# Transposes ahead of a run-time branch, one weight read later in the queue, two scalings on another engine

## The chip, the cores and the metric

The kernel runs on one core of one Trainium2 chip. The metric is the time of one launch in microseconds on the device. A run of the same kernel is repeated, and the median of the runs is the time that is compared. One further execution was recorded by the hardware profiler; all rows below come from it.

## The reference

The reference has three stages, each feeding the next.

1. Attention for 4 batches of 8 heads: 32 global queries look at all 544 keys, and 512 local queries look at the 32 global keys and at a window of 32 positions to either side. The result is 4 x 544 = 2,176 tokens of 512 numbers.
2. A mixture of 8 experts. For each token a gate picks one expert (or keeps the expert of the token before it, if a local gate says so). The token is multiplied by that expert's first weights (512 x 1024), passed through a relu, multiplied by the second weights (1024 x 512), and scaled by the softmax value of the expert.
3. A feed-forward layer for all tokens: 512 to 1024 with relu, a convolution of 3 taps along the sequence whose sigmoid gates the same values, and 1024 back to 512.

```python
for s in range(S):
    fresh_e = int(np.argmax(logits[b, s]))
    e = fresh_e if s == 0 or local_gate[b, s] < 0.5 else (prev_e if prev_e >= 0 else fresh_e)
    h = np.maximum(x[b, s] @ w1[e], 0.0)
    out[b, s] = p[e] * (h @ w2[e])
```

## The kernel before, in words

The order of the work on every engine is written out by hand; nothing is reordered by a scheduler. Each engine works through its own list, and waits on semaphores for what others must have done.

**Attention** (class `Attn`, L88) goes through 32 units (batch, block of 128 queries, half of the heads). At units 1 and 6 `warm` (L220) puts matmuls on a tile of zeros into TensorE's list; `WARM` says how many. They compute nothing that is used.

**The experts.** The tokens are sorted by expert into slots of 128 rows. Slots 0 and 1 are filled early, from the first half of the tokens; their work is the generator `fill`, whose steps are dealt out between the steps of the routing (`phase_b`, with the table `FILL`). From slot 2 (`NA`) on, `step(s)` (L1488) does one slot each: `small(s + 1)` reads a flag, `layer1(s)`, `fetch(s, 1)`, the gather of slot s + 3, `turn_x(s + 1)`, `resplit(s + 1, 1)`, `layer2(s - 1)`, `fetch(s - 1, 2)`, `turn_h(s)`, `resplit(s, 2)`. `last` (L1206) does the last slots and the first work of stage 3.

Products of weights and rows are made of three fp32r matmuls (high x high, high x low, low x high), so weights and rows are first split into a high and a low part. The weights of an expert are read to a staging tile (`W.s[1]` or `W.s[2]`, 2 MB each) and split by ACT and DVE (L1043, L1044).

A slot with at most 32 rows is "small": it skips the split and uses plain fp32 matmuls on the staging tile (`few_l1` L1434, `few_turn` L1441, `few_l2` L1450). Which it is, is known only at run time. `either` (L1379) therefore branches on a register that PE, ACT and DVE have loaded; small slots take the first arm, full slots the second.

`turn_x(s)` (L1385) transposes the 128 rows of a slot on PE (4 transposes of 128 x 128, L1393) into PSUM. In the small arm ACT copies the last 32 rows back (`raw`); in the full arm ACT and DVE split them (`split`). Before the change the four transposes stand in both arms.

`fetch(s, n)` (L1356) has SP read the weights that come after slot s: two register loads from `esi` (L1132; not repeated for n = 2 from slot 2 on), then a conditional DMA. Where the next slot has the same expert, the condition is false and the DMA moves nothing. Slots 0, 1 and 2 have the same expert here, so `fetch(1, 1)` and `fetch(1, 2)` move nothing, while `fetch(2, 1)` reads the next expert's first weights into the tile that slot 2's `few_l1` reads.

**Stage 3's first rows.** `load0` reads the first 544 rows, `scale0(i)` multiplies part i by its gate value (L1556 on DVE, L1554 on ACT), `xt0(i)` transposes the part (L1563) and splits it (L1565 on ACT, L1566 on DVE). Five parts are spread over `last`: parts 0 to 2 are scaled on DVE, parts 3 and 4 on ACT; `xt0(0)` and `xt0(1)` stand before the branch of the last slot's `few_turn`, `xt0(2)` to `xt0(4)` after it. `late` (L1266) is a register load on every engine, for the branch at L1191 that jumps over the slots that are rarely needed.

Of the kernel before, what the change touches and what calls it, by code (L numbers as in the profile page):

```python
# [8 lines left out]
F32 = mybir.dt.float32  # L9
# [3 lines left out]
AF = mybir.ActivationFunctionType  # L13
# [4 lines left out]
P = 128  # L18
# [23 lines left out]
V_JOBS = ({0: 3, 1: 3, 2: 2, 3: 2, 5: 2, 6: 3, 7: 3}, {0: 2, 5: 2, 6: 3, 7: 3}, {0: 2})  # L42
Q_EARLY = (6, 7, 13, 14, 15, 21, 22, 23)
SG_ACT = ()
WARM = {1: 2, 6: 1}


def win_order(v):
# [39 lines left out]
class Attn:  # L88
# [131 lines left out]
    def warm(self, n):  # L220
        if not n:
            return
        nc = self.nc
        t = self.ps.tile([P, 4, P], F32, tag="tr", name="wm")
        for k in range(n):
            nc.tensor.matmul(t, self.wz, self.wz[:, None, :].to_broadcast([P, 4, P]), start=True, stop=True)
# [763 lines left out]
SPLIT_B = {3: 5, 8: 6, 10: 7}  # L990
FILL = {1: 1, 3: 1, 6: 3, 7: 1, 8: 3, 9: 1, 10: 1, 11: 1, 12: 2, 13: 3, 15: 5, 16: 8}
HALF = 6
N_GLOB = 4
N_GS = 3
N_PUT = 5
# [55 lines left out]
class Moe:  # L1051
# [14 lines left out]
    def gather(self, s, pool=None):  # L1066
        xs = (pool or self.tp).tile([P, DM], F32, tag="xs", name="xs", bufs=NA if pool else 3)
        n = NTOK // 2 if pool else NTOK
        self.nc.gpsimd.indirect_dma_start(  # L1069
            out=xs, out_offset=None, in_=self.x_dram[0:n, :],  # L1070
            in_offset=bass.IndirectOffsetOnAxis(ap=self.rt.gidx[:, s:s + 1], axis=0),
            bounds_check=n - 1, oob_is_err=False)
        return xs

    def scatter(self, s, y):
        self.nc.gpsimd.indirect_dma_start(  # L1076
# [129 lines left out]
    def last(self, s, cwr, cw):  # L1206
        nc, W, f2, p = self.nc, self.W, self.f2, s - 1
        self.small(s)
        r = self.few_last = nc.values_load(self.rt.esi[0:1, 5, s:s + 1], min_val=0, max_val=1,
                                           engines=[mybir.EngineType.Activation, mybir.EngineType.DVE])  # L1210
        self.few_y_last = nc.values_load(self.rt.esi[0:1, 5, s:s + 1], min_val=0, max_val=1,
                                         engines=[mybir.EngineType.Activation])
        nc.scalar.activation(self.sig, self.sig, AF.Sigmoid)
        f2.load0()
        self.layer1(p)
        self.fetch(p, 1)
        self.turn_x(s)
        self.resplit(s, 1)
        x, xs, hp = self.xt.pop(s), self.xs.pop(s), self.h_tile()
        hs = self.tp.tile([P, FF], F32, tag="hs", name="hs")  # L1220
        ht = tuple(self.tp.tile([P, NFC, P], F32R, tag="g" + q, name="g" + q) for q in "hl")

        def split(a, b):
            for k in range(a, b):
                W.split_k(1, W.f, k, nc.vector)

        def resplit(a, b):
            with self.tc.If(self.chg[s] != 0):
                for k in range(a, b):
                    W.split_k(2, W.s, k, nc.vector)  # L1230

        self.conv_w(cwr, cw)
        with self.tc.If(r != 0):
            split(0, NKC)
        self.layer2(p - 1)
        self.fetch(p - 1, 2)
        self.rt.late_flag(s + 1, self.px.tile([P, 4, P], F32, tag="tr", name="lf")[0:1, 0, 0:1])
        for i in range(3):
            f2.scale0(i)
        self.turn_h(p)  # L1240
        self.resplit(p, 2)
        for i in range(3, 5):
            f2.scale0(i, True)
        with self.tc.If(self.sm[s] != 0):
            self.few_l1(xs, hp, hs)
        t = [self.ps.tile([P, 4, P], F32, tag="tr", name="hlp") for _ in range(2)]

        def full1():
            for k in range(NKC - 1):
                self.l1_mm(x, W.t[1], hp, k, range(2))  # L1250
            for c in range(2):
                self.l1_mm(x, W.t[1], hp, NKC - 1, (c,))
                self.relu_c(hp, hs, c)
            for a in (0, 4):
                for k in range(4):
                    nc.tensor.transpose(t[a // 4][:, k, :], hs[:, P * (a + k):P * (a + k) + P], self.ident)
                nc.scalar.copy(ht[0][:, a:a + 4], t[a // 4])
            for a in (0, 4):
                self.lo_t(ht, a, t[a // 4])
            split(0, NKC)  # L1260

        tq = self.px.tile([P, 4, P], F32, tag="tr", name="hlq")
        f2.xt0(0, self.px)
        f2.xt0(1, self.ps, "y")
        self.either(s, lambda: self.few_turn(hs, tq), full1)
        late = nc.values_load(self.rt.esi[0:1, 4, 1:2], min_val=0, max_val=P + 1)  # L1266
        for i in range(2, 5):
            f2.xt0(i, self.px if i == 3 else self.ps)
        self.layer2_out(p)
        self.fetch(p, 2)  # L1270
        resplit(0, 4)
        yp = hp[1]

        def full2():
            resplit(4, NFC)
            for k in range(NFC):
                self.l2_mm(ht, W.t[2], yp, k)

        with self.tc.If(self.sm[s] == 0) as c:
            full2()  # L1280
        with c.Else():
            self.few_l2(hs, yp, None)
        return yp, late
# [101 lines left out]
    def turn_x(self, s):  # L1385
        nc = self.nc
        xs = self.xs[s]
        x = self.xt[s] = tuple(self.tp.tile([P, NKC, P], F32R, tag="x" + q, name="x" + q) for q in "hl")
        t = (self.ps if s == NA else self.px).tile([P, 4, P], F32, tag="tr", name="xlp")

        def turn():
            for k in range(NKC):
                nc.tensor.transpose(t[:, k, :], xs[:, P * k:P * k + P], self.ident)  # L1393

        def few():
            turn()
            raw()

        def raw():
            nc.scalar.copy(xs[:, 0:NKC * TS].rearrange("p (k t) -> p k t", t=TS), t[:, :, P - TS:P])  # L1400

        def split():
            nc.scalar.copy(x[0], t)
            self.lo_t(x, 0, t)

        def full():
            turn()
            split()

        if s == NA:  # L1410
            turn()
            raw()
            split()
        else:
            self.either(s, few, full)

    def layer1(self, s):
        nc, W = self.nc, self.W
# [69 lines left out]
    def step(self, s):  # L1488
        W, hi = self.W, NSLOT - 2
        self.small(s + 1)  # L1490
        self.layer1(s)
        self.fetch(s, 1)
        if s + 3 < hi:
            self.xs[s + 3] = self.gather(s + 3)
        self.turn_x(s + 1)
        if s < NA + 16:
            self.raw_load(s - NA)
        self.resplit(s + 1, 1)
        if s == NA:
            x = self.f2.x_in[4]  # L1500
            self.rt.gates(x[:, 10:])
            self.rt.late_tokens(NSLOT - 5, x)
        if NA < s <= NA + 16:
            with self.tc.If(self.chg[s + 1] == 0):
                self.convert(s - NA - 1)
        if s == NA:
            for _ in self.rest:
                pass
        else:
            self.layer2(s - 1)  # L1510
            self.fetch(s - 1, 2)
        self.turn_h(s)
        self.resplit(s, 2)
        if NA < s <= NA + 16:
            with self.tc.If(self.chg[s + 1] != 0):
                self.convert(s - NA - 1)
# [15 lines left out]
class Ffn2:  # L1532
# [14 lines left out]
    def part0(self, i):  # L1547
        return (SG, 0, GT, 4) if i == 0 else (P, SG + P * i - P, i - 1, i - 1)

    def scale0(self, i, act=False):  # L1550
        n, _, j, a = self.part0(i)
        x, g = self.x_in[a][0:n], self.gate[0:n, j:j + 1]
        if act:
            self.nc.scalar.activation(x, x, AF.Copy, scale=g)  # L1554
        else:
            self.nc.vector.tensor_scalar(x, x, g, None, ALU.mult)  # L1556

    def xt0(self, i, ps, tag="tr"):
        nc = self.nc
# [225 lines left out]
def moe_kernel(ctx, tc, q_l, k_l, v_l, q_g, k_g, v_g, w_gate, w_local, w1, w2, w_in, conv_w, w_out, out):  # L1785
    nc = tc.nc
    outf = out.rearrange("b s d -> (b s) d")
    with tc.manual_schedule():
# [97 lines left out]
        with ExitStack() as c2:  # L1886
            rp = c2.enter_context(tc.tile_pool(name="r_tb", bufs=1))
            rs = c2.enter_context(tc.tile_pool(name="r_ps", bufs=1, space=PSUM))
            m.fetch(0, 1)
            for i, y in enumerate(rt.phase_b(rp, lambda shape, name: rs.tile(shape, F32, tag="rt", name=name))):  # L1890
                if y == "idx":
                    for s in range(NA, NA + 3):
                        m.xs[s] = m.gather(s)
                if i in SPLIT_B:
                    W.split_k(2, W.s, SPLIT_B[i], nc.vector)
                    if SPLIT_B[i] == NFC - 1:
                        m.fetch(0, 2)
                for _ in range(FILL.get(i, 0)):
                    next(fill)
            m.fetch(1, 1)  # L1900
            while next(fill) != "turn":
                pass
            m.turn_x(NA)
            m.resplit(NA, 1)
            while next(fill) != "half":
                pass
            m.rest = fill
            m.fetch(1, 2)
            m.small(NA)
        m.px = moe_ctx.enter_context(tc.tile_pool(name="m_px", bufs=2, space=PSUM))  # L1910
        xa.close()
# [36 lines left out]
```

## Time and profile before

| what | value |
|---|---|
| median of 3 runs | 604.5 us (604.38, 604.5, 609.06) |
| profiled execution | 602.84 us, of which the recorded span is 601.1 us |
| PE busy | 565.3 us (94%) |
| DVE, ACT, POOL busy | 392.3 (65%), 335.2 (56%), 171.1 us (28%) |
| granted TensorE clock over the span | 0.997 of full speed |
| instructions | 16418 |

The span runs from the first to the last recorded instruction; 1.74 us of the profiled execution lie around it. The share of busy time is a mean over stages: attention ends at about 148 us, the experts run to about 396 us, stage 3 from there to the end. Idle time of an engine matters only where that engine's next work sets the time of the stage.

### The profile page before, as it was taken

To read this page: it belongs to the slowest core of one execution; us is meant where nothing else is said; L and a number is where in the kernel's file an instruction comes from. 1 tells how busy PE (TensorE), PEld (TensorE's weight loads), DVE (VectorE), ACT (ScalarE), POOL (GpSimd) and SP (SyncE) were. 2 spreads that over 40 slices of the span, in tenths; PEclk is the share of its full clock that TensorE was granted. 3 is DMA by queue.
4 is the path that set the end of the run, shared out by engine and by line. 5 is a ranking of instruction groups with operands and counts; after the bars stand their busy time and mean duration, and the time that the engine had idled before them with its cause. 6 is when DMAs were issued, how large, how long until landed. Compare 5 with 4: busy or idle time off the path is not lost. (4 is left out here: it accounts for less than half of the span.)

```text
span 601.1 us, 16418 instructions
## 1 busy us (share of the span) xinstructions
PE 565.3 (94%) x6086; PEld 469.7 (78%) x6086; DVE 392.3 (65%) x815; ACT 335.2 (56%) x663; POOL 171.1 (28%) x226
## 2 busy tenths in 40 slices
PE   8788889889898999999999999889999999999997
PEld 5566667666666888888787788679988998998986
DVE  7878686876964857786487884637972664473430
ACT  4765555566224745865676775747853563553331
POOL 8656740034021422343142441010321502300100
PEclk9999999999999999999999999989999999999999
DMA  9998959567228964597366784313010210000001
GB/s 235 218 218 222 222 148 203 190 216 240 107 61 275 346 213 154 186 358 246 102 251 228 251 306 133 138 44 102 19 35 36 71 36 35 19 19 19 36 36 53
DMA packets 60644, 90.57 MB, mean 151 GB/s; under 512 B 25726, under 2 KB 34198, under 8 KB 60504
## 3 DMA queue, kind: packets, MB, share of 16 engines
q1 hardware_dynamic: 57016, 78.93, 42.8%
q0 software_dynamic: 3520, 10.23, 5.0%
q8 instruction: 64, 1.05, 0.7%
q14 instruction: 44, 0.36, 0.2%
HBM read 125.87 MB, written 15.79 MB: 236 GB/s over the span
## 5 line engine op out<-in xcount | busy, mean ns | idle before, releaser
L1651 DVE SCALAR_TENSOR_TENSOR fc<-f_hp,cw,fc 128x544 f32<-128x544 f32 (+2 forms) x66 | 51.6, 782 | 79.1 <-ACT fc L1649 77.7
L1044 DVE TENSOR_TENSOR wl<-ws,wh 128x512 fp32r<-128x512 f32 (+1 forms) x80 | 65.1, 875 | 17.6 <-ACT wh L1043 15.9
L1043 ACT CAST wh<-ws 128x512 fp32r<-128x512 f32 (+1 forms) x84 | 57.9, 773 | 4.3 <-DMA ws<-in_moe_w_dram 3.3
L1120 PE MATMUL yp<-wh,gh 128*128 128x512 f32 x136 | 54.9, 404 | 0.2 <-ACT gh L1092 0.2
L1709 PE MATMUL f<-wh,fh 128*128 128x512 f32 (+1 forms) x144 | 54.8, 380 | 0.0
L1120 PE MATMUL yp<-wl,gh 128*128 128x512 f32 x136 | 53.7, 395 | 1.0 <-DVEq L1371 0.6
L1709 PE MATMUL f<-wh,fl 128*128 128x512 f32 (+1 forms) x144 | 54.5, 378 | 0.0
L1709 PE MATMUL f<-wl,fh 128*128 128x512 f32 (+1 forms) x144 | 54.4, 378 | 0.0
L1120 PE MATMUL yp<-wh,gl 128*128 128x512 f32 x136 | 53.4, 393 | 0.3 <-DVE gl L1096 0.3
L1076 POOL DMA_INDIRECT y_dram<-ys,sidx x22 | 25.5, 1157 | 92.5 <-ACT ys L1483 29.9
L278 ACT ACTIVATE pr<-sp,nm 128x128 f32<-128x128 f32 x128 | 36.6, 376 | 24.0 <-DVE nm L275 24.0
L1104 PE MATMUL hp<-wh,xh 128*128 128x512 f32 x136 | 45.3, 405 | 2.3 <-ACT wh L1043 1.4
L1069 POOL DMA_INDIRECT xs<-x_dram,gidx x22 | 24.5, 1112 | 69.5 <-ACT pr L278 34.4
L1104 PE MATMUL hp<-wl,xh 128*128 128x512 f32 x136 | 43.6, 393 | 0.3 <-DVE wl L1044 0.2
L1104 PE MATMUL hp<-wh,xl 128*128 128x512 f32 x136 | 43.7, 393 | 0.0
L1656 ACT ACTIVATE f_hp<-f 128x544 f32<-128x544 f32 x31 | 19.4, 626 | 39.2 <-PE f L1632 39.2
L1349 ACT ACTIVATE hs<-hp 128x512 f32<-128x512 f32 x34 | 18.7, 596 | 38.7 <-PE hp L1104 37.7
L1017 POOL TENSOR_TENSOR wf<-wf,fx 128x512 int32<-128x512 int32 x16 | 20.9, 1307 | 59.2 <-DVE wf L1016 54.0
L1718 ACT COPY fy<-f 128x512 f32<-128x512 f32 (+1 forms) x18 | 10.1, 564 | 46.0 <-PE f L1709 46.0
L1709 PEld LDWEIGHTS f<-wh,fl 128*128 128x128 f32 x144 | 27.1, 188 | 5.1
L1120 PEld LDWEIGHTS yp<-wl,gh 128*128 128x128 f32 x136 | 25.6, 188 | 7.1 <-DVEq L1371 1.5
L1709 PEld LDWEIGHTS f<-wl,fh 128*128 128x128 f32 x144 | 27.1, 188 | 4.6
(388 smaller groups left out, 1502.6 us busy)
## 6 DMA issues: line engine op xcount, KB each, us to landing
ws<-in_moe_w_dram SPq DMA_DIRECT2D x42, 2048.0 KB
fx<-y_dram SPq DMA_DIRECT2D x17, 256.0 KB
raw<-in_k_l_dram SPq DMA_DIRECT2D x16, 256.0 KB
x_dram<-x SPq DMA_DIRECT2D x16, 256.0 KB
fx<-in_moe_w_in_dram SPq DMA_DIRECT2D x8, 512.0 KB
fx<-in_moe_w_out_dram SPq DMA_DIRECT2D x8, 512.0 KB
out_dram<-fy SPq DMA_DIRECT2D x16, 256.0 KB
VA<-in_v_l_dram SPq DMA_DIRECT2D x20, 192.0 KB
```

The costliest lines, as they stand in the source:

```text
L278: nc.scalar.activation(pr[:, hp, :], sp[:, hp, :], AF.Exp, bias=nm[:, hp:hp + 1], scale=-1.0)
L1017: nc.gpsimd.tensor_tensor(a, a, lo, ALU.add)
L1043: (cp.tensor_copy if cp else self.nc.scalar.copy)(h, src[n][:, k, :])
L1044: eng.tensor_tensor(l, src[n][:, k, :], h.bitcast(F32), ALU.subtract)
L1069: self.nc.gpsimd.indirect_dma_start(out=xs, out_offset=None, in_=self.x_dram[0:n, :], in_offset=bass.IndirectOffsetOnAxis(ap=self.rt.gidx[ ...
L1076: self.nc.gpsimd.indirect_dma_start(out=self.y_dram[:, :], out_offset=bass.IndirectOffsetOnAxis(ap=self.rt.sidx[:, s:s + 1], axis=0), in_= ...
L1104: self.nc.tensor.matmul(hp[c], a[:, k, :], b[:, 512 * c:512 * c + 512], start=k == 0 and m == 0, stop=k == NKC - 1 and m == 2)
L1120: self.nc.tensor.matmul(yp, a[:, k, :], b, start=k == 0 and m == 0, stop=k == NFC - 1 and m == 2)
L1349: self.nc.scalar.activation(hs[:, 512 * c:512 * c + 512], hp[c], AF.Relu)
L1651: nc.vector.scalar_tensor_tensor(c[:, a:b], hp[:, a + t:b + t], self.cw[:, t, f:f + 1], c[:, a:b], ALU.mult, ALU.add)
L1656: self.nc.scalar.activation(hp[:, 1:S + 1].rearrange("p (a c) -> p a c", a=2), p[:, :, 0:272], AF.Relu)
L1709: self.nc.tensor.matmul(yp[:, cs], x[:, c], w[:, cs], start=f == 0 and n == 0, stop=f == NFC - 1 and n == 2)
```

## The change

Six edits:

- `WARM`: one matmul on zeros more at unit 1 (3 for 2) and at unit 6 (2 for 1) of the attention.
- `WARM_B`: after step 6 of `phase_b` the new `Moe.warm` puts 4 fp32r matmuls of 128 x 512 into PE's list. They write a tile of the "y" kind (PSUM, two buffers) that nothing reads.
- `last`: parts 3 and 4 of the first rows are scaled on DVE, behind the branch of `few_turn`; before, ACT scaled them ahead of `few_l1`.
- `last`: `xt0(1)` stands behind that branch, together with parts 2 to 4.
- `turn_x`: the four transposes stand once, ahead of the branch; the arms hold only the copies.
- `fetch(1, 2)` stands in `step(2)` behind the rest of `fill`, where later slots have their `fetch(s - 1, 2)`; before, it stood ahead of slot 2, between `fetch(1, 1)` and `fetch(2, 1)`.

```diff
-WARM = {1: 2, 6: 1}
+WARM = {1: 3, 6: 2}
...
+WARM_B = 6
...
+    def warm(self, n):
+        t = self.ps.tile([P, DM], F32, tag="y", name="wm")
+        for _ in range(n):
+            self.nc.tensor.matmul(t, self.W.t[1][0][0][:, 0:P], self.W.t[1][0][0][:, 0:512], start=True, stop=True)
...
         self.turn_h(p)
         self.resplit(p, 2)
-        for i in range(3, 5):
-            f2.scale0(i, True)
         with self.tc.If(self.sm[s] != 0):
             self.few_l1(xs, hp, hs)
...
         f2.xt0(0, self.px)
-        f2.xt0(1, self.ps, "y")
         self.either(s, lambda: self.few_turn(hs, tq), full1)
+        for i in range(3, 5):
+            f2.scale0(i)
         late = nc.values_load(self.rt.esi[0:1, 4, 1:2], min_val=0, max_val=P + 1)
-        for i in range(2, 5):
-            f2.xt0(i, self.px if i == 3 else self.ps)
+        for i in range(1, 5):
+            f2.xt0(i, self.px if i == 3 else self.ps, "y" if i == 1 else "tr")
         self.layer2_out(p)
...
-        def turn():
-            for k in range(NKC):
-                nc.tensor.transpose(t[:, k, :], xs[:, P * k:P * k + P], self.ident)
-
-        def few():
-            turn()
-            raw()
+        for k in range(NKC):
+            nc.tensor.transpose(t[:, k, :], xs[:, P * k:P * k + P], self.ident)
...
-        def full():
-            turn()
-            split()
-
         if s == NA:
-            turn()
             raw()
             split()
         else:
-            self.either(s, few, full)
+            self.either(s, raw, split)
...
         if s == NA:
             for _ in self.rest:
                 pass
+            self.fetch(1, 2)
         else:
...
-    def scale0(self, i, act=False):
+    def scale0(self, i):
         n, _, j, a = self.part0(i)
-        x, g = self.x_in[a][0:n], self.gate[0:n, j:j + 1]
-        if act:
-            self.nc.scalar.activation(x, x, AF.Copy, scale=g)
-        else:
-            self.nc.vector.tensor_scalar(x, x, g, None, ALU.mult)
+        x = self.x_in[a][0:n]
+        self.nc.vector.tensor_scalar(x, x, self.gate[0:n, j:j + 1], None, ALU.mult)
...
                 for _ in range(FILL.get(i, 0)):
                     next(fill)
+                if i == WARM_B:
+                    m.warm(4)
...
             m.rest = fill
-            m.fetch(1, 2)
             m.small(NA)
```

## Rows read from the trace of the kernel before

**Rows 1.** The page's slices: tenths of full TensorE clock in 40 equal slices.
```profile
PEclk9999999999999999999999999989999999999999
```
**Rows 2.** Windows: length, each engine's busy us (instructions), granted clock, DMA share, GB/s.
```profile
200.00:250.00 50.00, 50.00 (x245) 41.62 (x244) 35.67 (x56) 31.54 (x55) 16.70 (x14) 1.00 0.61 217
```
**Rows 3.** Timeline of PE, slots 2 to 4: start us, us, instruction, [idle before, releaser].
```profile
177.06 1.93 PE L1434 MATMUL hp<-ws,xs 128*32 128x256 f32 x32 [0.25 <-DMA ws<-in_moe_w_dram]
...
191.85 0.73 PE L1104 MATMUL hp<-wh,xh 128*128 128x512 f32 x2 [1.38 <-ACT wh L1043]
```
**Rows 4.** Timeline of SP's DMA issues in the same stretch: three fetches one by one.
```profile
176.86 0.08 SPq L1036 DMA_DIRECT2D ws<-in_moe_w_dram  x1
...
178.46 0.07 SPq L1036 DMA_DIRECT2D ws<-in_moe_w_dram  x1
...
180.14 0.38 SPq L1036 DMA_DIRECT2D ws<-in_moe_w_dram  x1
```
**Rows 5.** Timeline of ACT in the same stretch.
```profile
190.76 3.89 ACT L1043 CAST wh<-ws 128x1024 fp32r<-128x1024 f32 x4 [2.52 <-DMA ws<-in_moe_w_dram]
```
**Rows 6.** Timeline of PE through `last` to the first matmul of stage 3.
```profile
381.98 1.93 PE L1434 MATMUL hp<-ws,xs 128*32 128x256 f32 x32
...
385.68 0.41 PE L1441 MATMUL hlq<-ident,hs 128*128 128x128 f32 x2 [0.81 <-ACT hs L1436]
387.11 1.50 PE L1563 MATMUL f_tr<-ident,fx 128*128 128x128 f32 x12 [1.02 <-DVEq L1380]
388.36 0.49 PE L1120 MATMUL yp<-wh,gh 128*128 128x512 f32 x1
...
398.80 0.36 PE L1632 MATMUL f<-f_x0h,wh 128*128 128x272 f32 x1 [2.45 <-PEq L1191]
```
**Rows 7.** Timeline of ACT in `last`.
```profile
383.93 1.33 ACT L1554 ACTIVATE fx<-fx,gate 128x512 f32<-128x512 f32 x2 [1.20 <-DMA fx<-y_dram]
385.17 0.36 ACT L1436 ACTIVATE hs<-hp 128x256 f32<-128x256 f32 x1
```
**Rows 8.** Timeline of DVE in `last`: the three scalings.
```profile
382.28 1.26 DVE L1556 TENSOR_SCALAR fx<-fx,gate 32x512 f32<-32x512 f32 x3
```
**Rows 9.** PE's sequencer at L1266 and at L1191: min/median/max ns, first to last start.
```profile
L1266 PEldq TENSOR_LOAD <-esi x1: 302/302/302, 385.9 to 385.9; - x1
...
L1191 PEldq COMPARE_BRANCH  x1: 2970/2970/2970, 395.5 to 395.5; - x1
```
**Rows 10.** Timeline of PE in the attention: the two `warm` places and a later wait.
```profile
13.60 1.98 PE L226 MATMUL wm<-wz 128*128 128x512 f32 x4
...
36.01 1.12 PE L226 MATMUL wm<-wz 128*128 128x512 f32 x2 [0.71 <-ACT pg L380]
...
48.39 0.66 PE L173 MATMUL trp<-ident,nat 128*128 128x128 f32 x4 [1.75 <-POOL nat L166]
```
**Rows 11.** Timeline of POOL in the attention: the first of the copies that precede it.
```profile
37.80 3.03 POOL L218 COPY VB<-VA 32x1560 f32<-32x1560 f32 x2 [2.81 <-DMA VA<-in_v_l_dram]
```
**Rows 12.** Timeline of PE in `phase_b`, behind step 6.
```profile
154.95 0.25 PE L725 MATMUL r_ep<-c_idb,r_er 2*128 2x2 bf16 x4 [1.09 <-DVE r_er L719]
```
**Rows 13.** Timeline of PE: transposes and matmuls at a branch behind a full slot.
```profile
203.84 1.03 PE L1469 MATMUL hlp<-ident,hs 128*128 128x128 f32 x8
204.63 0.72 PE L1104 MATMUL hp<-wh,xh 128*128 128x512 f32 x2
205.18 0.62 PE L1104 MATMUL hp<-wh,xl 128*128 128x512 f32 x2
```
**Rows 14.** The same place behind a small slot's second layer.
```profile
342.51 1.06 PE L1469 MATMUL hlp<-ident,hs 128*128 128x128 f32 x8
343.71 0.70 PE L1104 MATMUL hp<-wh,xh 128*128 128x512 f32 x2
```
**Rows 15.** Groups by line: count, busy us, mean ns, idle us before them.
```profile
L1393 PE MATMUL xlp<-ident,xs 128*128 128x128 f32 x80 | 12.2, 274 | 0.0
```
**Rows 16.** A window behind the jump at L1191, columns as in rows 2.
```profile
399.00:403.00 4.00, 4.00 (x21) 4.00 (x21) 0.00 (x0) 0.00 (x0) 1.24 (x7) 0.57 0.05 13
```

## The prediction

> **What bounds the kernel now.** I started with the page's slices: TensorE's clock is granted in full in every slice but one [rows 1]. The windows then show where PE sets the time: in the 50 us of rows 2 PE is busy for all 50.00 us, while DVE, ACT and DMA are not, so between slots a gain must come from PE's own list. I went on to the timeline of PE and looked for the few places where PE stands still, since an edit can only win there. The change touches three: the start of slot 4, where PE waits 1.38 us for ACT [rows 3], which itself waits for a DMA [rows 5]; the middle of `last`, where PE waits 0.81 us for ACT and 1.02 us for DVE [rows 6]; and the jump at L1191, after which stage 3 starts [rows 6, 9]. The attention is different: there PE waits for others (1.75 us for POOL [rows 10]), and added PE work can hide.
>
> **The sum's base.** Durations come from the profiled execution, 602.84 us with a span of 601.1 us and 1.74 us around it. That is 1.7 us under the median of 604.5 us; I carry the difference over to the median.
>
> **The later read of second weights.** `fetch(1, 1)`, `fetch(1, 2)` and `fetch(2, 1)` are issued at 176.86, 178.46 and 180.14 [rows 4]. The first two last 0.08 and 0.07 us and move nothing, but each needs two register loads first: from one issue to the next are 1.60 and 1.68 us. `fetch(2, 1)` may go once `few_l1` of slot 2 has read its tile, at 177.06 + 1.93 = 178.99 [rows 3]. Without `fetch(1, 2)` ahead of it, SP's registers are ready at 176.86 + 1.68 = 178.54, so PE sets the issue: 178.99 and a little for the semaphore, 179.15 as an estimate. That is 1.0 us earlier than 180.14. The read is what ACT waits for (2.52 us [rows 5]) and ACT is what PE waits for, so the 1.0 us come off PE's 1.38 us; 0.4 us of the wait remain. From there on PE is full [rows 2] and carries the gain along. Bounds: 1.15 us (issue at the very end of `few_l1`), and nothing, if something else holds the issue at 180.14. The moved fetch now stands on SP behind `fetch(2, 1)` and the raw read that follows; the next issue that needs SP's registers, `fetch(3, 1)`, cannot go before `fetch(2, 1)` has landed, some 10 us later (180.14 to 190.76 [rows 4, 5]), so the two loads of 1.6 us are hidden there. If that cover were gone, ACT's split would start 1.6 us later. PE's `few_l2` of slot 2 waits for the moved fetch too; slot 3's first layer, 24 matmuls of 0.28 us [rows 13] or 6.7 us, lies ahead of it, so it does not feel it. On POOL nothing is moved: the gather and the rest of `fill` that the fetch now follows are on other engines' lists than SP's.
>
> **The first rows' scalings.** ACT spends 1.33 us on two scalings and only then, at 385.17, evacuates `few_l1` [rows 7], which PE finished at 381.98 + 1.93 = 383.91 [rows 6]. Without them ACT can start at about 384.05 and end at 384.4; `few_turn` on PE, now at 385.68, can start at about 384.55: 1.1 us earlier. Behind it PE loads a register (0.2 us after `few_turn`, 0.30 us and a little for the use [rows 9]; 0.85 us together as an estimate), so the transposes start at about 385.4. PE now waits there until 387.11 because DVE has to pass the same branch [rows 6]; in the new order DVE's last work ahead of the branch is part 0 alone, and it is through at about 385.2. What PE then issues is 16 transposes for the 12 of before: 12 take 388.36 - 387.11 = 1.25 us [rows 6], so 16 take 1.67 us, and the second layer of the slot before starts at 387.1 instead of 388.36: 1.2 us earlier. The scalings themselves cost DVE 1.26 / 3 = 0.42 us each [rows 8], 0.84 us from 385.25 to 386.1, in time for parts 3 and 4, which PE reaches at 386.25 and 386.7. Behind them on DVE stands the split of part 1, which waits for ACT's copy of it until about 386.6 anyway. Next in line is ACT: it must copy four parts instead of three behind the branch, and is done at about 388.2, just when the second layer's first chunk lets it split weights. There is no slack left there, so I keep as bounds 1.3 us and 0.3 us. From the second layer to stage 3's first matmul at 398.80 lie PE's own matmuls and the jump of 2.97 us [rows 9], so the gain passes through.
>
> **The transposes ahead of the branch.** The instructions on PE stay the same in number for every slot that is run, and PE branches on the same register as before. All 80 transposes of L1393 found PE without any idle time before them: 0.0 us [rows 15]. There is no wait to win, so I take 0. At one kind of place a branch does show: behind 8 transposes the next matmul normally starts after 204.63 - 203.84 = 0.79 us [rows 13], but after 343.71 - 342.51 = 1.20 us where a small slot's second layer went before and PE's sequencer had no work queued up [rows 14]. So a bare branch is worth 0.41 us. With the transposes moved, a branch that had stood between them and the matmuls stands directly ahead of the next one. If that were never covered, 19 slots would pay 19 x 0.41 = 7.8 us; if it freed such a branch at a small slot, that would be 0.41 us for each of them. I take 0 since the full slots show no gap at any branch.
>
> **The matmuls on zeros.** In the attention each costs about 1 us: two took 1.98 us, one 1.12 us [rows 10]. Two more are 2.1 us at most. Later PE waits 1.75 us for POOL at 48.39 [rows 10], and POOL's copies start at 37.80, when a read of `VA` lands [rows 11], which no matmul sets; so most is swallowed. I take +0.2 us, with bounds of 0 and +2.1. In `phase_b` four fp32r matmuls take 4 x 0.28 = 1.1 us (two start 205.18 - 204.63 = 0.55 us apart from the next [rows 13]), and the place holds 1.09 us of idle PE, ended by DVE [rows 12]. I take 0, with a bound of +1.1 if that wait were gone. The y buffer that they take only swaps the turn of the two buffers.
>
> On the other side stands what such matmuls might buy. [...] In the attention and in `phase_b` the row shows full clock [rows 1], so by the rows there is nothing to buy. [...]
>
> **The sum.** -1.0 (read) - 1.2 (scalings) + 0 (transposes) + 0.2 + 0 (zeros) = -2.0 us: 600.8 us for a profiled execution, 602.5 us for the median.
>
> **Rivals.**
> 1. *The waits are replaced.* SP's issue is held by something else, and in `last` ACT's fourth copy delays the weights' split. For it: ACT's time there comes out with no slack. Against: rows 4 show SP at register loads alone. Then the gain is 0.3 us and the zeros cost 0.2 to 0.5: 604.5 us, the change doing nothing.
> [...]
> 3. *Bare branches* (slower). Behind each hoisted group of transposes, between them and the next layer's matmuls, PE's sequencer passes two branches with too little queued. It decides as soon as the queued matmuls run out first. Price 19 x 0.41 = 7.8 us, less the 2.0: 604.5 + 5.8 = 610.3 us. Against: rows 15. [...]
> 4. *The zeros are not swallowed*: +2.1 and +1.1 instead of 0.2, 605.5 us.
>
> **Numbers.** Chances: the forecast 0.55 (its own range 601.3 to 603.8), rival 1 0.18, rival 2 0.15, rival 3 0.05, rival 4 0.07. The range from 599.6 to 606.0 takes in rivals 1, 4 and most of 2, and leaves out about 2 in 10 with rival 3 and a median that falls on a run like that of 609.06 us. About 1%, 6 us, is what a measurement tells from no change. Faster than 598.5 us needs three falls of the clock (0.05); slower than 610.5 needs rival 3 in full and no gain elsewhere (0.03); within 1% 0.92.
>
> **What would show it.** The read: `fetch(2, 1)` at about 179.2 on the old time axis, ACT's first split about 1 us earlier, PE's wait at slot 4 near 0.4 us. The scalings: no L1554 on ACT, the 0.81 us wait gone, the second layer in `last` about 3.2 us behind the end of `few_l1` instead of 388.36 - 383.91 = 4.45. The transposes: still no idle time before them, and full PE windows between slots. The zeros: `trp` at 48.39 no more than 0.2 us later. Wrong I would be if PE's idle time between slots grew, or if the jump to stage 3 took more than 2.97 us.

## The result and the profile after

The median fell from 604.44 to 598.57 us (598.09, 598.38, 598.76, 599.04): a ratio of 0.9887, 95% interval 0.9837 to 0.9936. The profiled executions differ by 4.75 us (602.84 to 598.09; spans 601.1 to 596.3 us). On another chip the same pair gave 605.02 and 601.48 us, 0.9938 [0.9908, 0.9969]. So the change makes the kernel some 0.6 to 1.1% faster, and the forecast of 602.5 us (599.6 to 606.0) was too high. Ratios and their intervals are estimated from the fast runs alone and need not equal the quotient of the medians beside them.

The comparison that I read first lays the same instruction of PE (TensorE's matmuls) of both traces side by side and notes how much earlier it starts after the change:

| place on PE | before, us | after, us | earlier by |
|---|---|---|---|
| start of slot 2's `few_l1` (end of attention and routing) | 177.06 | 176.67 | 0.39 |
| transposes of slot 5 | 197.80 | 196.80 | 1.00 |
| transposes of slot 10, the last ahead of a loss | 255.84 | 254.82 | 1.02 |
| transposes of slot 12 | 277.08 | 276.49 | 0.59 |
| `few_l1` in `last` | 381.98 | 381.43 | 0.55 |
| second layer in `last` | 388.36 | 386.67 | 1.69 |
| first matmul of stage 3 | 398.80 | 395.15 | 3.65 |
| next transposes in stage 3 | 415.41 | 410.24 | 5.17 |

The last two steps are the surprise: 1.96 us at the jump to stage 3 (the lead grows from 1.69 to 3.65 us) and 1.52 us right behind it (to 5.17), where no edit touches an instruction. They are 3.5 of the 4.75 us. From there to PE's last matmul the lead stays at 5.1 us; the tail behind that is 0.3 us longer.

Timeline of PE in the kernel after, from `few_l1` in `last` to stage 3 (answers to [rows 6]):
```profile
381.43 1.93 PE L1429 MATMUL hp<-ws,xs 128*32 128x256 f32 x32
...
383.96 0.41 PE L1436 MATMUL hlq<-ident,hs 128*128 128x128 f32 x2 [0.23 <-ACT hs L1431]
384.83 2.08 PE L1556 MATMUL f_tr<-ident,fx 128*128 128x128 f32 x16 [0.46 <-issue]
386.67 0.48 PE L1126 MATMUL yp<-wh,gh 128*128 128x512 f32 x1
...
392.69 1.95 PE L1445 MATMUL hp<-ws,hs 128*32 128x128 f32 x64 [0.28 <-ACT wh L1044]
...
395.15 0.36 PE L1625 MATMUL f<-f_x0h,wh 128*128 128x272 f32 x1 [0.51 <-DVEq L1208]
```
The waits of 0.81 and 1.02 us in `last` are now 0.23 and 0.46, and the wait ahead of stage 3 is 0.51 instead of 2.45. PE's sequencer at the same jump (now L1197; [rows 9]), and a window behind it, columns as in [rows 2] (answers to [rows 16]):
```profile
L1197 PEldq COMPARE_BRANCH  x1: 330/330/330, 393.8 to 393.8; - x1
```
```profile
395.20:399.20 4.00, 4.00 (x32) 4.00 (x33) 0.00 (x0) 1.70 (x6) 0.76 (x1) 1.00 0.20 70
```
The jump takes 330 ns for 2970, and behind it the clock is granted in full, 1.00 for 0.57. The long branch has not vanished, though. The sequencer at the slots' branches (L1385) shows one that the kernel before does not have (its longest there is 431 ns), and PE's timeline beside it shows what it cost:
```profile
L1385 PEldq COMPARE_BRANCH  x94: 68/207/3704, 175.0 to 386.2; - x94
```
```profile
260.79 0.38 PE L1436 MATMUL hlp<-ident,hs 128*128 128x128 f32 x2
262.02 0.70 PE L1110 MATMUL hp<-wh,xh 128*128 128x512 f32 x2 [0.85 <-ACT hs L1437]
```
The 3704 ns start at 257.2 us, in slot 9, while PE still has matmuls of the slot before in its queue up to 260.8. So they seem to cost only 0.43 us (1.02 to 0.59 in the table); the run after_shift24 below agrees.

### The profile page after: what moved, and what is told of

The parts are those of the page before. It is cut to its first block, busy times and chain, and to the rows that moved or that the text cites. A ratio compares the mean times of both kernels' runs of the same rounds, so it can differ in the third digit from the quotient of the medians.

```text
span 596.3 us, 16441 instructions
## 1 busy us (share of the span) xinstructions
PE 565.8 (95%) x6094; PEld 469.9 (79%) x6094; DVE 391.7 (66%) x817; ACT 333.9 (56%) x661; POOL 171.6 (29%) x226
## 5 line engine op out<-in xcount | busy, mean ns | idle before, releaser
L1110 PEld LDWEIGHTS hp<-wh,xl 128*128 128x128 f32 x136 | 25.4, 188 | 6.9 <-DVE xl L1102 0.9
```

Source lines behind the costliest of these rows:

```text
L1110: self.nc.tensor.matmul(hp[c], a[:, k, :], b[:, 512 * c:512 * c + 512], start=k == 0 and m == 0, stop=k == NKC - 1 and m == 2)
```

## The experiments

**Theory A**: the jump's 2.97 us hang on where the jump stands in PE's program. The hoist (the transposes put ahead of the branch) takes 8 instructions per slot out of the program (not out of what is executed) and so moved the jump. The runs ask only whether the place decides, not why it should. At stake are about 1.9 us of PE's idle time (2.45 us before, 0.51 after) and, with the fall of the clock in [rows 16], 4 x (1 - 0.57) = 1.7 us more. **Rival B**: the jump got short through `last`'s edit, by timing. **Rival C**: the matmuls on zeros hold the clock.

To place the jump I counted PE's program: a matmul is two instructions (weight load and matmul), a plain fp32 one four. If the count is divided into blocks of 256 from an offset chosen to fit, the 77 taken branches of L1380 in the trace of the kernel before part cleanly: the 13 that pass a block's boundary take 292 to 431 ns, the 64 others 169 to 224. Of all block sizes from 96 to 599 instructions, only 256, 257 and 258 split them so. In the trace of the kernel after, the same division holds for 74 of 77. A "block boundary" is no more than that here: a place in the count at which the branches get longer. Some ten neighbouring offsets fit, so a position is good to about ten instructions; the differences between kernels are better known. Positions below are "instructions behind the last boundary".

To move code without changing what is executed, transposes are added in the arm of a branch that this slot never takes (slots 20 and 3 are full slots). hoist_dead12 and dead20 are single runs; the others were timed against the kernel before on the same chip. There its own runs lay between 598.9 and 609.7 us, so ratios are wide, and sizes of a microsecond are read from the traces.

**dead60**, on the kernel before:
```diff
         def few():
             turn()
             raw()
+            if s == 20:
+                for _ in range(60):
+                    nc.tensor.transpose(t[:, 0, :], xs[:, 0:P], self.ident)
```


> The kernel before, with 60 more transposes in the small arm of turn_x(20). Slot 20 is a full slot, so none of them is executed: only the place in PE's program of all that follows moves by about 120 instructions, to where it stands in the kernel after (counted from a block boundary every 256 instructions, the jump to stage 3 stood 21 behind one and now stands about 142 behind one, as in the kernel after). [...] Rival B (the jump got short through last's edit and its timing): jump 2970 ns, clock falls, time as before. Rival C (matmuls on zeros keep the clock): time as before.

Measured: 601.33 against 605.49 us, 0.9914 [0.9882, 0.9945]. PE's sequencer and PE:
```profile
L1191 PEldq COMPARE_BRANCH  x1: 345/345/345, 397.6 to 397.6; - x1
```
```profile
396.46 1.95 PE L1453 MATMUL hp<-ws,hs 128*32 128x128 f32 x64 [0.28 <-ACT wh L1043]
398.75 0.36 PE L1635 MATMUL f<-f_x0h,wh 128*128 128x272 f32 x1 [0.34 <-PEq L1191]
```
Theory A had put the jump at some 330 ns here, PE's idle time at about 0.5 us and the gain at 3.6 us. Instructions that never run give most of the whole change's gain. Of the three, only A forecast that.

**after_dead68**, the other way round, on the kernel after:
```diff
         def raw():
             nc.scalar.copy(...)
+            if s == 20:
+                for _ in range(68):
+                    nc.tensor.transpose(t[:, 0, :], xs[:, 0:P], self.ident)
```


> The kernel after, with 68 more transposes in the small arm of turn_x(20), which slot 20 never executes. They put the jump to stage 3 back to where it stood before (about 23 instructions behind a block boundary, 21 in the kernel before, 142 in the kernel after); every edit of the change stays. Theory A: the jump takes about 3 us again, PE idles about 2.5 us before stage 3, the clock falls behind it: +1.9 + 1.7 = +3.6 us against the kernel after, about 602.2 us, 0.995 to 0.997 of before. Rival B (last's edit shortens the jump) and rival C (the zeros hold the clock): as the kernel after, 598.6 us.

Measured: 603.85 us, 0.9961 [0.9929, 0.9993]. The jump, PE behind it and two windows:
```profile
L1197 PEldq COMPARE_BRANCH  x1: 3030/3030/3030, 398.1 to 398.1; - x1
```
```profile
397.01 1.95 PE L1448 MATMUL hp<-ws,hs 128*32 128x128 f32 x64 [0.28 <-ACT wh L1044]
401.62 0.36 PE L1628 MATMUL f<-f_x0h,wh 128*128 128x272 f32 x1 [2.66 <-PEq L1197]
```
```profile
402.00:404.00 2.00, 2.00 (x14) 2.00 (x14) 0.00 (x0) 0.00 (x0) 1.24 (x7) 0.76 0.03 4
404.00:406.00 2.00, 2.00 (x10) 2.00 (x10) 0.00 (x0) 0.00 (x0) 0.00 (x0) 0.50 0.04 13
```
Every edit is in, zeros too, and the long jump, the idle PE and the fall of the clock are all back. B falls, and so does C for the fall behind the jump.

**hoist**, the kernel before with the hoisted transposes alone:
```diff
-        def turn():
+        for k in range(NKC):
...
-            self.either(s, few, full)
+            self.either(s, raw, split)
```


> The kernel before with the four transposes of turn_x ahead of the branch and nothing else of the change. No PE instruction that is executed is added or taken away, but 8 per slot leave the program (the copy in the other arm), so that the jump to stage 3 stands about 125 instructions behind a block boundary instead of 21. Theory A: jump about 330 ns, PE waits about 0.5 us there, no fall of the clock: -3.6 us (0.994). One new long branch of some 3 us may show at a small slot, mostly hidden by queued matmuls (up to +0.5). Rival B: jump 2970 ns, time as before to 0.3 us. Rival C: clock falls, time as before.

Measured: 603.44 us, 0.9974 [0.9943, 1.0005]. A missed here: 125 behind a boundary the jump is still long, if shorter. (The trace also has a new branch of 2990 ns at slot 9, which the expectation allowed for.)
```profile
L1191 PEldq COMPARE_BRANCH  x1: 2383/2383/2383, 397.5 to 397.5; - x1
```
```profile
396.26 2.08 PE L1440 MATMUL hp<-ws,hs 128*32 128x128 f32 x64 [0.28 <-ACT wh L1043]
400.19 0.36 PE L1622 MATMUL f<-f_x0h,wh 128*128 128x272 f32 x1 [1.85 <-PEq L1191]
```
The last 128 instructions ahead of the jump are `few_l2` (64 weight loads and 64 matmuls in the trace), and the first of them wait for ACT (in the kernel before PE idles 0.28 us there; the weight loads, 0.68 us). I call that the hold. In the kernels with a long jump the last boundary lies behind it, 21 to 125 instructions ahead of the jump; in those with a short one it lies ahead of it, at 142. From the start of `few_l2`, before the change at
```profile
394.39 1.95 PE L1450 MATMUL hp<-ws,hs 128*32 128x128 f32 x64 [0.28 <-ACT wh L1043]
```
to the end of the long jump it is 398.47 - 394.39 = 4.1 us before, 3.6 us here, 4.1 in after_dead68. So theory A was sharpened: the jump is short if the last boundary lies ahead of `few_l2`, at least 128 instructions ahead of the jump, and long if it lies behind the hold. Two single runs test it. Their times, 605.35 and 599.45 us, say nothing by themselves: the kernel before took 598.86 to 608.89 us on that chip.

**hoist_dead12**: the hoist with 12 transposes in `raw` of slot 20.

> The kernel with only the hoisted transposes, plus 12 transposes in the small arm of turn_x(20), never executed. In the run of the hoist alone the jump still took 2383 ns, 125 instructions behind a block boundary; in three runs with 142 behind one it took 330 to 345 ns. [...] Here the jump stands 150 behind: about 330 ns, PE idle about 0.4 us before stage 3 (1.85 with the hoist alone). If the hoist itself were what left the jump long: 2.4 us.

Measured: the jump is short.
```profile
L1191 PEldq COMPARE_BRANCH  x1: 330/330/330, 400.8 to 400.8; - x1
```
But PE still waits 1.12 us instead of 0.4, that is 0.8 us more than in dead60 (0.34).

**dead20**: as dead60, with 20.

> The kernel before with 20 more transposes in the small arm of turn_x(20), never executed; the jump stands about 62 instructions behind a block boundary (21 in the kernel before: 2970 ns; 125 with the hoist: 2383 ns; 142: 330 to 345 ns). Theory A, sharpened: the boundary lies behind the hold at few_l2, so the jump stays long, between 2.4 and 3.0 us, and PE waits about 2.2 us. If any shift of the code mends the jump: about 330 ns.

Measured: the jump stays long, and PE idles 2.56 us, both a little more than expected.
```profile
L1191 PEldq COMPARE_BRANCH  x1: 3078/3078/3078, 393.5 to 393.5; - x1
```
So not every shift mends the jump, as the sharpened theory said.

**last_only**: `last`'s two edits on the kernel before.
```diff
-        for i in range(3, 5):
-            f2.scale0(i, True)
...
-        f2.xt0(1, self.ps, "y")
         self.either(s, lambda: self.few_turn(hs, tq), full1)
+        for i in range(3, 5):
+            f2.scale0(i)
```


> The kernel before with the two edits of last alone (parts 3 and 4 scaled on DVE behind the branch, the transposes of part 1 behind it). The jump to stage 3 stands where it stood (22 instructions behind a block boundary). Theory A: -1.1 us up to the second layer of the slot before, jump still about 3 us, clock still falls, so -1.1 in all (603.3 us, 0.998). Rival B: jump short as in the kernel after, clock full: -1.1 - 3.6 = -4.7 us (0.992). Rival C: -1.1.

Measured: 606.15 us, 1.0 [0.9968, 1.0031]; the gain of 1.1 us is below what these runs resolve. The trace shows it, and the jump as long as ever:
```profile
390.38 1.93 PE L1433 MATMUL hp<-ws,xs 128*32 128x256 f32 x32
...
395.65 0.50 PE L1120 MATMUL yp<-wh,gh 128*128 128x512 f32 x1
...
406.55 0.36 PE L1631 MATMUL f<-f_x0h,wh 128*128 128x272 f32 x1 [2.92 <-PEq L1191]
```
From the end of `few_l1` to the second layer it is 395.65 - 392.31 = 3.34 us, for 4.45 before [rows 6]. B falls a second time. The clock, though, did not fall behind this jump. (The profiled execution is the slowest of the ten, 609.42 us, with 0.982 of the clock over its span: the clock fell earlier, to 0.94 over the first 170 us.)

**fetch_only**: `fetch(1, 2)` behind the rest of `fill`, on the kernel before.

> The kernel before with fetch(1, 2) moved behind the rest of fill and nothing else. The jump stands where it stood (21 behind a block boundary). My step of the prediction: fetch(2, 1) 1.0 us earlier against few_l1 of slot 2, PE's wait at slot 4's first layer 1.38 - 1.0 = 0.4 us, jump still about 3 us; -1.0 us (0.998). The comparison of the two traces gave 0.6 us for the stretch. If something else holds the read: wait 1.4 us, 0.

Measured: 603.84 us, 0.9978 [0.9955, 1.0001]. Timeline of PE, SP and ACT around slot 4:
```profile
177.96 1.93 PE L1434 MATMUL hp<-ws,xs 128*32 128x256 f32 x32 [0.23 <-DMA ws<-in_moe_w_dram]
...
191.52 0.73 PE L1104 MATMUL hp<-wh,xh 128*128 128x512 f32 x2 [0.45 <-ACT wh L1043]
```
```profile
180.10 0.38 SPq L1036 DMA_DIRECT2D ws<-in_moe_w_dram  x1
```
The read goes out 2.14 us behind the start of `few_l1`, for 3.08 before, and PE's wait is 0.45 for 1.38. The jump takes 2975 ns.

**after_again, after_shift24, after_nozero**, on one chip with fetch_only. The second puts 24 transposes into `raw` of slot 3; the third sets the numbers of zeros back and puts 8 there:
```diff
-WARM = {1: 3, 6: 2}
+WARM = {1: 2, 6: 1}
...
-                if i == WARM_B:
-                    m.warm(4)
```


> The kernel after once more, for comparison on the same chip as the next three. All theories: 0.989 of before, inside 0.984 to 0.994; jump 330 ns; a branch of some 3.7 us at slot 9 (257 us).

> The kernel after, with 24 more transposes in the small arm of turn_x(3), which slot 3 never executes. All code from slot 3 on moves by 48 instructions of PE, so slot 9's branches stand where they stood in the kernel before, and the jump to stage 3 stands 191 behind a block boundary instead of 142. Theory A: slot 9's branch takes about 180 ns instead of 3.7 us, PE's first layer of slot 10 starts 0.4 to 0.8 us earlier, the jump stays near 330 ns: 0.5 us faster than the kernel after (0.988 of before). Rivals B and C: as the kernel after, with the long branch at slot 9 still there.

> The kernel after without its six more matmuls on zeros (WARM and WARM_B as before), and with 8 transposes in the small arm of turn_x(3), never executed, that put the code behind them back in place (jump 143 instructions behind a block boundary, 142 in the kernel after). Theory A: jump 330 ns, clock full at stage 3's start, time as the kernel after to 0.4 us. Rival C (the zeros hold the clock): a fall of the clock in the attention or behind the jump, +1.7 us or more. That the zeros cost time: -0.2 to -1 us.

Measured: 601.48 us, 0.9938 [0.9908, 0.9969]; 599.2 us, 0.9909 [0.9878, 0.9939]; 599.98 us, 0.9926 [0.9894, 0.9957]. The times cannot be told apart. The branches of L1385, first the shifted kernel's, then that without zeros:
```profile
L1385 PEldq COMPARE_BRANCH  x94: 68/207/476, 176.7 to 387.1; - x94
```
```profile
L1385 PEldq COMPARE_BRANCH  x94: 68/207/4151, 179.4 to 390.7; - x94
```
Slot 9's long branch goes away with a shift of 48 instructions, as A says. A branch of 2.8 to 4.2 us stands at slot 9 in every traced kernel with the hoist whose slot 9 stands about where the kernel after has it (six of them), and in none of the other seven. From slot 4's first layer to `last` the shifted kernel takes 382.30 - 192.12 = 190.18 us, the kernel after 381.43 - 190.84 = 190.59: 0.41 us less, about the 0.43 that slot 9 seemed to cost. Without the added zeros the jump is short (330 ns) and the clock behind it 1.00, so the zeros are not what holds the clock there. For the rest of the kernel the trace alone would speak for C: its clock falls three times before slot 2 (0.990 over the span), which the expectation had named as a sign of C. But the granted clock of all its seven runs has a median of 0.996, against 0.9935 for the twelve of after_again with the zeros and 0.994 for the 24 of the kernel before. So the runs do not show that the zeros hold the clock anywhere.

**shift32_nozero**: both of the last two together, as a candidate for the best.

> The kernel after without its six more matmuls on zeros, with 32 transposes in the small arm of turn_x(3), never executed, so that slot 9's branches stand as in the kernel before and the jump 191 behind a block boundary. Theory A: no branch over 0.5 us, jump 330 ns, clock full behind it; as the kernel after with 24 such transposes, 0.4 us faster than the kernel after, 0.990 of before on the same chip. Rival C (the zeros hold the clock): slower than that by 1.7 us or more.

Measured: 599.66 against 605.49 us, 0.9937 [0.9908, 0.9966]; no slot branch over 430 ns, jump 329 ns. Yet PE waits 1.35 us ahead of stage 3, as in hoist_dead12 (1.12). It is no better than the kernel after as far as these runs tell.

All traces in one table (the clock is that of the 4 us from PE's first matmul of stage 3 on, to 0.2 us):

| kernel | jump stands behind a boundary by | jump, ns | PE idle ahead of stage 3, us | clock in the 4 us behind |
|---|---|---|---|---|
| before | 21 | 2970 | 2.45 | 0.57 |
| fetch_only | 21 | 2975 | 2.46 | 0.65 |
| last_only | 22 | 3290 | 2.92 | 1.00 |
| after_dead68 | 23 | 3030 | 2.66 | 0.68 |
| dead20 | 62 | 3078 | 2.56 | 1.00 |
| hoist | 125 | 2383 | 1.85 | 1.00 |
| dead60 | 142 | 345 | 0.34 | 1.00 |
| after | 142 | 330 | 0.51 | 1.00 |
| after_again | 142 | 334 | 0.51 | 1.00 |
| after_nozero | 143 | 330 | 0.52 | 1.00 |
| hoist_dead12 | 150 | 330 | 1.12 | 1.00 |
| after_shift24 | 191 | 329 | 0.52 | 1.00 |
| shift32_nozero | 191 | 329 | 1.35 | 1.00 |

## Why the prediction was wrong

**The step that failed** is "From the second layer to stage 3's first matmul at 398.80 lie PE's own matmuls and the jump of 2.97 us [rows 9], so the gain passes through." I took the jump's duration as a property of the jump. It hangs on the place in the program at which it stands (2970 ns at 21 behind a boundary, 345 at 142 in dead60), and the change moves that place. I had written that the hoist leaves the instructions on PE the same in number "for every slot that is run"; true, but the copy that is not run leaves the program. My own sign for error ("if the jump ... took more than 2.97") looked one way only. Worth: 1.96 us at the jump, whose cause dead60 and after_dead68 show, and 1.52 us of clock behind it in this pair of traces.

**The clock** of [rows 16] I booked as staying. The chances of the prediction count in falls of the clock (rival 2, and three falls for a time under 598.5 us), at 1.7 us each. No run shows that every fall costs that: the one behind the jump cost 4 x (1 - 0.57) = 1.7 us by [rows 16] and 1.52 us by the pair of traces, and the one in the attention, below, shows no cost. The fall that went is the one behind the jump. In the attention the kernel after even has one that the kernel before does not, in a window behind a wait of 2.73 us for a DMA:
```profile
45.65 0.41 PE L234 MATMUL trg<-ident,gn 128*128 128x128 f32 x2 [2.73 <-DMA gn<-in_k_g_dram]
```
```profile
44.00:50.00 6.00, 3.93 (x50) 3.34 (x50) 4.96 (x11) 2.87 (x9) 5.76 (x6) 0.76 0.74 212
```
PE is not full in that stretch (3.93 of 6 us busy), and the attention still ends 0.39 us earlier, so no cost of this fall shows. Both traces have 0.997 of the clock over the span; a mean clock hides that the fall in stage 3, where PE is full, cost 1.52 us, and that the other shows no cost in this pair.

That the other was free is not shown to hold for such falls in general. Of the 26 runs of the kernel before on dead60's chip, the eight with the lowest granted clock (0.988 and 0.989) have a median of 607.16 us, the five with the highest (0.996 and 0.997) one of 602.94. That is a connection and not a trial, but it would fit medians that lie above the profiled execution by falls of the clock. The zeros are not shown to change it. On the chip of after_again both kernels had the same mean clock (0.993), and the change still gained 605.02 - 601.48 = 3.5 us: about what the account below gives without its clock term. So the jump is the part of the surprise that stays, and the 1.52 us of clock may in part be luck of this pair.

**The later read**: right in its mechanism, but 0.6 us for the predicted 1.0. SP issues `fetch(2, 1)` 178.81 - 176.67 = 2.14 us behind the start of `few_l1`, 0.94 earlier than before (predicted 1.0), and 0.21 us behind the end of `few_l1` (estimated 0.16):
```profile
178.81 0.38 SPq L1037 DMA_DIRECT2D ws<-in_moe_w_dram  x1
```
```profile
190.84 0.73 PE L1110 MATMUL hp<-wh,xh 128*128 128x512 f32 x2 [1.08 <-ACT wh L1044]
```
PE got 0.6 us of it here, since this read took ACT 0.3 us longer to get (178.81 to 189.75; 10.94 us for 10.62, [rows 4, 5]); in fetch_only, where it took 10.32, PE got 1.2. PE's wait is still 1.08 us and not 0.4, because PE itself also reaches it 0.3 us earlier behind `few_l1`.

**The scalings**: right. 386.67 - 383.36 = 3.31 us from `few_l1` to the second layer, predicted 3.2; 1.1 us gained for 1.2, and 1.1 again in last_only. DVE's two scalings take 0.88 us for 0.84. They start 385.28 - 383.36 = 1.92 us behind `few_l1`, not the predicted 385.25 - 383.91 = 1.34, PE's transposes start 384.83 - 383.96 = 0.87 us behind `few_turn` (estimated 0.85), and the 16 take 386.67 - 384.83 = 1.84 us for 1.67:
```profile
385.28 0.88 DVE L1549 TENSOR_SCALAR fx<-fx,gate 128x512 f32<-128x512 f32 x2 [0.41 <-DVEq L1385]
```

**The hoisted transposes**: no wait at them, as said (0.0 again, the row that answers to [rows 15]), and rival 3's bare branches did not come. What the transposes did to the code behind them I did not look for.
```profile
L1397 PE MATMUL xlp<-ident,xs 128*128 128x128 f32 x80 | 12.2, 275 | 0.0
```
I had the 2.97 us of one branch before me [rows 9], and asked what a branch costs only for the branches that the hoist lays bare, not for the code that it shifts.

**The zeros**: swallowed as far as this pair tells, better than +0.2. The wait for POOL shrank to 0.42 us and that in `phase_b` to 0.16 ([rows 10, 12]):
```profile
48.22 1.12 PE L173 MATMUL trp<-ident,nat 128*128 128x128 f32 x4 [0.42 <-POOL nat L166]
...
154.56 0.25 PE L725 MATMUL r_ep<-c_idb,r_er 2*128 2x2 bf16 x4 [0.16 <-DVE r_er L719]
```
The 0.39 us by which slot 2 starts earlier are no proof of a gain: in the traces without a fall of the clock ahead of it, slot 2 starts anywhere from 177.06 (before) to 179.66 us (after_dead68).

**The account** of the traces: 0.39 (attention and routing) + 0.61 (read) + 1.14 (`last`, 0.55 to 1.69) + 1.96 (jump) + 1.52 (clock) - 0.43 (slot 9) = 5.2 us, less 0.3 of tail. The medians differ by 1.1 us more, because the profiled execution of before lay 604.44 - 602.84 = 1.6 us under its median and that of after only 598.57 - 598.09 = 0.5 us; that part has no trace.

**Open**: why the place of a branch decides how long it takes; why PE waits 0.8 us more behind a short jump in hoist_dead12 and shift32_nozero, the latter with the jump at the same place as in after_shift24; and when the clock falls.

## What to carry to other kernels

A branch that takes microseconds in a trace need not be a fixed cost: the jump here took 2383 to 3290 ns at some places in PE's program and 329 to 345 ns at others. Ask where the branch stands, and expect any edit that adds or removes code ahead of it, run or not, to move it. An edit that "executes nothing new" can therefore win or lose more than its own operations; add never-executed instructions to the kernel before, up to the new place, and see whether that alone gives the gain. Price a fall of the clock by the stage in which it lies, from the trace: the one behind the jump cost 1.52 us, the one in the attention shows no cost, and over the 26 runs of the kernel before a low clock and a long time go together (medians of 607.16 and 602.94 us).

## What the runs showed of the hardware that I had not expected

- In the trace of before, the taken branches of L1380 on PE's sequencer take about 0.2 us (169 to 224 ns), and 0.29 to 0.43 us where they pass a block boundary of the count. A few took much longer: the jump 2.4 to 3.3 us, a branch at slot 9 2.8 to 4.2 us. Why they take longer was not shown.
- At the jump the long branch ends 3.6 us (hoist) to 4.4 us (last_only) after `few_l2` starts, in the trace of before 4.1 us, with little DMA traffic (a share of 0.22 over these 4.1 us). At slot 9 of the kernel after, the long branch ends at 260.9, 7.5 us after the start of an earlier one of 293 ns (253.4 us), while the weights are read (below; the next to last number is the DMA share). Whether that traffic plays a part was not tried.
```profile
257.00:261.00 4.00, 4.00 (x20) 3.22 (x18) 3.21 (x6) 1.41 (x2) 2.10 (x2) 1.00 1.01 330
```
- The clock fell behind the jump in three of the five traces in which PE had idled 2.45 us or more (2.45, 2.46 and 2.66, not at 2.56 and 2.92), and in none of the eight with 1.85 us or less. In after_dead68 two whole microseconds went at 0.50. So a fall can follow idle time of this length, and does not always; what brings it about was not shown.
